# Gated linear attention and GLU in one kernel: chunks of 128 tokens, and the low parts on VectorE

## The chip, the cores and the metric

The kernel runs on one core of a Trainium2 chip. The metric is the device time of one execution of the whole program, in microseconds (us). The kernel before takes 612.56 us, the median of three runs (611.88 to 612.68).

The core's engines each follow their own list of instructions and wait for one another by semaphores: TensorE (PE in the profile; its weight loads have a row of their own, PEld), VectorE (DVE), ScalarE (ACT), GpSimd (POOL), and SyncE (SP), which here only starts transfers. SBUF is the memory that all engines use; PSUM holds what TensorE accumulates, in eight banks of 128 partitions x 512 words.

## The reference

Four sequences of 768 tokens, eight heads of 48 channels. Each head carries a 48 x 48 state through its sequence; what comes out is the input of a gated linear unit.

```python
for t in range(S):
    state = alpha[:, :, t, :, None] * state + np.einsum('bhd,bhe->bhde', k[:, :, t], v[:, :, t])
    y[:, :, t] = np.einsum('bhd,bhde->bhe', q[:, :, t], state)
...
x = attn_out.transpose(0, 2, 1, 3).reshape(B * S, H * D)      # 3072 x 384
gate = 1.0 / (1.0 + np.exp(-(x @ w_gate)))                    # 384 x 1536
val = x @ w_val
return (gate * val @ w_out)                                   # 1536 x 384
```

All inputs are float32. The kernel receives the weights as float64 words with the same values.

## The kernel before

**Groups, steps and units.** The 3072 tokens are six groups of T = 512. The GLU of a group has 12 **steps**, one for each 128 of the 1536 inner channels, so there are 72 (`step`, L507). The attention of a group has four **units**, one for each pair of heads, so there are 24 (`unit`, L340). A pair of heads lies on the 128 partitions, one head in the lower and one in the upper half, 48 of 64 partitions each.

**A step.** Every product with weights is done three times, on a high and a low part of each factor in a rounded 32-bit format (`products`, L198; `PAIRS`): high x high, high x low, low x high. TensorE makes pg and pv (gate and value, nine matmuls of 512 columns each, L202), and later po (L526), nine more: six with hh, three with hl. Between them ACT makes the sigmoid of pg (L512, tile sg), DVE multiplies it with pv (L513, into sg), ACT rounds that to the high part hh (L515), and POOL subtracts for the low part hl (L518). PSUM has one bank for pg, one for pv, three for po (they accumulate over the 12 steps of a group) and three, called at, for the units.

**A unit.** It works in chunks of C = 64 tokens, so a group has CH = 8 of them. The input tile (in, one DMA from `rows`) holds decay factors, k and q by channel; va and vb hold v of the two heads. DVE scans the decays backwards (G, L357) and forwards (F, L361), with small operations between (L359, L360, L363); POOL makes k x G (L365), and DVE and POOL make q x F (L375, tiles xa and xb); ACT sums |F| for an overflow flag (L377). TensorE then does four things, 16 matmuls each unless said otherwise: it turns k over (L387, a product with the identity; ACT copies it out as kn, L392), makes the scores of each chunk (L399; DVE masks them, L415), makes what each chunk adds to the state (L406; DVE chains the states chunk by chunk, L431), and makes the outputs. In groups 2 to 5 each output is one matmul (L470) over a stacked factor: the masked scores and q x F lie in two halves of the partitions of xa and xb, and v and the scaled states (L439, POOL) in those of va and vb. In groups 0 and 1 (`apart`) the two terms are separate matmuls (L457, L461). ACT and DVE make the parts of y (L476, L477), and a DMA puts them into x (L485).

**Weights.** A weight piece comes in by DMA and is split in six operations (`weight_piece`, L298): ACT scales the upper words (L312) and makes exponent and upper fraction bits in the 16-bit half words (L313), DVE takes the sign by half words (L315) and shifts in the lower bits (L317), ACT makes the high part (L319), POOL the low part (L321). There are 25 pieces, three for the first of the 12 weight blocks and two for each other one.

**What sets the order.** All of this goes into a planner (`Plan`, L42) as parts: engine, modelled time, key, and what it reads and writes. `order` (L71) plays the parts through by these times and picks, on each engine, the ready part with the lowest key. What it finds is each engine's fixed order of instructions. The keys follow the step at which a part is wanted. Rings of buffers (`Ring`, L127) set how far a unit can run ahead: two input tiles, two hh and hl, one sg. WARM = 60 matmuls (L497) without use stand at the start.

Of the kernel before, what the change touches and what calls it, by code (L numbers as in the profile page):

```python
# [8 lines left out]
F32 = mybir.dt.float32  # L9
# [11 lines left out]
C = 64  # L21
# [20 lines left out]
class Plan:  # L42
# [13 lines left out]
    def add(self, engine, time, key, fn, reads=(), writes=()):  # L56
# [12 lines left out]
        self.parts.append((engine, time, key, fn, deps))  # L69

    def order(self):  # L71
# [12 lines left out]
        begun, memory, busy = [None] * len(self.parts), 0.0, {}  # L84
        for _ in self.parts:
            best = None
            for e, ns in waiting.items():
                if not ns:
                    continue
                t = max(free[e], min(ready_at[n] for n in ns))  # L90
                n = min((n for n in ns if ready_at[n] <= t + 1e-9), key=lambda n: (self.parts[n][2], n))
                if best is None or t < best[0]:
                    best = (t, n)
# [14 lines left out]
            free[engine] = done  # L108
            if engine != "tensor" and data is not None:
# [48 lines left out]
RATE = 225e3  # L158
# [10 lines left out]
def act(n):  # L169
    return 0.09 + n / 1180  # L170
# [35 lines left out]
def chunked(ctx, tc, rows, vc, weights_in, out, const, ident, flags, weights, within):  # L206
# [45 lines left out]
    r_va = ring("va", 2, CH, D, early=[borrow("w8", CH, D) for _ in range(2)])  # L252
    r_vb = ring("vb", 2, CH, D, early=[borrow("w8", CH, D) for _ in range(2)])
# [5 lines left out]
    r_kn = ring("kn", 1, CH, D, early=[borrow("w6", CH, D) for _ in range(2)])  # L259
    r_sd = ring("sd", 1, CH, D, early=[borrow("w6", CH, D) for _ in range(2)] + [borrow("w7", CH, D)])  # L260
    r_yt = ring("yt", 2, 2, T, dtype=F32R)
    r_xa = ring("xa", 2, T, early=[borrow("x1", T), borrow("w7", T)])
    r_xb = ring("xb", 2, T, early=[borrow("x1", T), borrow("w7", T)])
# [22 lines left out]
    for half in range(2):  # L286
        m = mask[half * C:(half + 1) * C]
        nc.gpsimd.affine_select(out=m, in_=m, pattern=[[1, C]], compare_op=ALU.is_ge,
                                fill=0.0, base=0, channel_multiplier=-1)
    for r, lo in ((r_va, 0), (r_vb, C)):  # L290
        for _, t in r.tiles + r.early:
            nc.vector.memset(t[lo:lo + C], 0.0)
# [5 lines left out]
    def weight_piece(f, key):  # L298
        cuts = (0, DM, 2 * DM, WF) if f == 0 else (0, WF // 2, WF)
        over = before(f"w{f}") if f >= 6 else []  # L300
        for i, (lo, hi) in enumerate(zip(cuts, cuts[1:])):
# [4 lines left out]
            half = raw.bitcast(U16).rearrange("p m (w h) -> p m w h", h=2)  # L306
            ru, rl = (rn, "u"), (rn, "l")
            up = upper.bitcast(F32)
# [3 lines left out]
            plan.add("scalar", act(n), kk, lambda up=up: nc.scalar.activation(out=up, in_=up, func=AF.Copy, scale=2.0 ** -112), writes=[ru])  # L312
            plan.add("scalar", 0.09 + n / 500, kk, lambda half=half: nc.scalar.activation(  # L313
                out=half[:, :, 0, 0], in_=half[:, :, 0, 1], func=AF.Copy, scale=2.0 ** -13, bias=2.0 ** -15 - 0.5), writes=[rl])
            plan.add("vector", 0.1 + n / 770, kk, lambda half=half: nc.vector.tensor_scalar(  # L315
                out=half[:, :, 0, 1], in0=half[:, :, 1, 1], scalar1=0x8000, scalar2=None, op0=ALU.bitwise_and), [ru], [rl])
            plan.add("vector", 0.07 + n / 860, kk, lambda upper=upper, lower=lower: nc.vector.scalar_tensor_tensor(  # L317
                out=lower, in0=upper, scalar=3, in1=lower, op0=ALU.logical_shift_left, op1=ALU.bitwise_or), [ru], [rl])
            plan.add("scalar", act(n), kk, lambda lower=lower, lo=lo, hi=hi: nc.scalar.copy(  # L319
                out=weights.tile(f)[:, 0, lo:hi], in_=lower.bitcast(F32)), [rl], [("wh", f, i), *over])  # L320
            plan.add("gpsimd", pool_(n), kk, lambda lower=lower, lo=lo, hi=hi: nc.gpsimd.tensor_tensor(  # L321
                out=weights.tile(f)[:, 1, lo:hi], in0=lower.bitcast(F32), in1=weights.tile(f)[:, 0, lo:hi], op=ALU.subtract),
                [rl, ("wh", f, i)], [("w", f, i)])
# [16 lines left out]
    def unit(u, g, p, t):  # L340

        n, nch = T, CH
        apart = u < 2 * NP
        bank = r_bank if u < NP else r_at
        inn, tin = r_in.next()
        for lo, hi, marks in ((0, A_K, "a"), (A_K, WIDTH, "rk")) if u < 2 else ((0, WIDTH, "ark"),):
# [228 lines left out]
    for g in range(NG):  # L575
        if 2 <= g + 1 < NG:
            units(g + 1)
# [156 lines left out]
```

## Time and profile before

| | |
|---|---|
| median of three runs | 612.56 us |
| profiled execution | 612.03 us |
| its span, first to last instruction | 610.3 us |
| TensorE clock granted, mean over the span | 0.988 of full |
| moved by DMA | 52.94 MB, mean 87 GB/s |
| of the chain of work that ended last | PE 83%, DVE 8%, POOL 3%, ACT 3%, issue 2% |

The busy time of an engine in the page counts its instructions, and for TensorE the ends of matmuls are modelled. The page also cuts the span into 40 slices of 15.26 us and gives the busy share of each in tenths:

```profile
PE   7985989889999999999999999999999999999995
DVE  7875799799961535534534535525535312101111
ACT  1374775856342122132122132122132122212121
```

One reads them as a course of events: TensorE is not quite full for the first ten slices, while DVE and ACT split the weights and the units of the first two groups are made; after that TensorE is full and the others repeat a pattern of three slices.

### The profile page before, as it was taken

What the parts mean: (1) busy time and instruction counts of PE and PEld (TensorE: products, weight loads), DVE (VectorE), ACT (ScalarE), POOL (GpSimd) and SP (SyncE); (2) the same over time, 40 slices, a digit from 0 to 9 for tenths busy, and PEclk for the clock granted to TensorE, in tenths of its full rate; (3) what the DMA queues carried; (4) which work ended last, traced back from release to release, by engine and by line L of the source; (5) the groups of instructions that cost most, each with busy time, mean ns of one, the idle gap of its engine ahead of it and who ended that gap; (6) DMA issues with size and microseconds to landing.
All of it is one profiled execution on the core that took longest, in us unless ns stands there. A gap on an engine that the chain in (4) does not pass through costs nothing.

```text
span 610.3 us, 12631 instructions
## 1 busy us (share of the span) xinstructions
PE 583.8 (96%) x5334; PEld 464.9 (76%) x5334; DVE 307.3 (50%) x536; ACT 200.1 (33%) x331; POOL 266.4 (44%) x241
## 2 busy tenths in 40 slices
PE   7985989889999999999999999999999999999995
PEld 3754767677788888888888888888888888888784
DVE  7875799799961535534534535525535312101111
ACT  1374775856342122132122132122132122212121
POOL 4556586687771425425434425425424312212110
PEclk9997999999999999999999999999999999999998
DMA  8466465463440130240330240330340110110001
GB/s 269 131 178 231 133 188 183 147 197 116 145 118 0 53 92 8 85 144 6 87 92 6 88 144 2 91 92 2 93 143 2 40 27 1 38 41 0 1 2 58
DMA packets 17107, 52.94 MB, mean 87 GB/s; under 512 B 2832, under 2 KB 5904, under 8 KB 17040
## 3 DMA queue, kind: packets, MB, share of 16 engines
q1 hardware_dynamic: 17040, 52.03, 28.3%
q8 instruction: 44, 0.72, 0.5%
q14 instruction: 23, 0.19, 0.1%
HBM read 37.86 MB, written 4.72 MB: 70 GB/s over the span
## 4 chain that ended last, share of the span: by engine, by line
PE 83%; DVE 8%; POOL 3%; ACT 3%; issue 2%; DVEq 0%; POOLq 0%; ACTq 0%
PE po L526 23%; PE pg L202 22%; PE pv L202 22%; PE at L399 3%; PE at L387 3%; PE at L470 3%; PE at L406 3%; DVE first_w L315 1%; DVE first_w L317 1%; PE pv L497 1%; POOL w L321 1%; ACT raw L313 1%; DVE G L357 1%; DVE raw L315 1%; POOL xa L375 1%
## 5 line engine op out<-in xcount | busy, mean ns | idle before, releaser
L202 PE MATMUL pg<-x,w 128*128 128x512 f32 x648 | 166.0, 400 | 10.0 <-ACT sg L512 4.8
L518 POOL TENSOR_TENSOR hl<-sg,hh 128x512 fp32r<-128x512 f32 x71 | 97.8, 1377 | 156.5 <-ACT hh L515 155.4
L202 PE MATMUL pv<-x,w 128*128 128x512 f32 x648 | 160.2, 391 | 0.0
L202 PEld LDWEIGHTS pg<-x,w 128*128 128x128 f32 x648 | 122.4, 191 | 40.1 <-ACT sg L512 4.9
L513 DVE TENSOR_TENSOR sg<-pv,sg 128x512 f32<-128x512 f32 x72 | 49.5, 687 | 194.8 <-PE pv L202 189.2
L202 PEld LDWEIGHTS pv<-x,w 128*128 128x128 f32 x648 | 120.9, 188 | 26.6 <-DVE sg L513 0.8
L526 PE MATMUL po<-hh,w 128*128 128x512 f32 x432 | 116.7, 404 | 0.3 <-ACT hh L515 0.3
L512 ACT ACTIVATE sg<-pg 128x512 f32<-128x512 f32 x72 | 43.6, 605 | 187.8 <-PE pg L202 181.0
L526 PEld LDWEIGHTS po<-hh,w 128*128 128x128 f32 x432 | 78.6, 188 | 19.4 <-ACT hh L515 1.2
L515 ACT CAST hh<-sg 128x512 fp32r<-128x512 f32 x72 | 44.8, 622 | 113.1 <-DVE sg L513 113.1
L526 PE MATMUL po<-hl,w 128*128 128x512 f32 x216 | 62.9, 398 | 2.2 <-POOL hl L518 2.2
L365 POOL TENSOR_TENSOR in<-in,G 128x512 f32<-128x512 f32 x22 | 28.3, 1288 | 70.3 <-DVE G L357 64.2
L357 DVE TENSOR_TENSOR_SCAN G<-in,d1g 128x512 f32<-128x512 f32 x22 | 30.4, 1384 | 52.4 <-DMA in<-in_rows_dram 52.3
L375 POOL TENSOR_TENSOR xb<-in,F 64x512 f32<-64x512 f32 x16 | 26.9, 1684 | 57.3 <-PE at L470 54.3
L526 PEld LDWEIGHTS po<-hl,w 128*128 128x128 f32 x216 | 40.2, 188 | 13.3 <-POOL hl L518 3.8
L431 DVE SCALAR_TENSOR_TENSOR st<-st,dec,at 128x48 f32<-128x48 f32 x176 | 46.2, 263 | 7.4 <-PE at L406 2.0
L361 DVE TENSOR_TENSOR_SCAN F<-in,d1f 128x512 f32<-128x512 f32 x22 | 37.0, 1680 | 1.5
L321 POOL TENSOR_TENSOR w<-raw,w 128x576 fp32r<-128x576 f32 (+1 forms) x14 | 23.5, 1682 | 10.8 <-ACT w L319 10.5
L476 ACT CAST yt<-at 128x512 fp32r<-128x512 f32 x22 | 13.0, 592 | 46.2 <-PE at L470 40.7
L387 PE MATMUL at<-ident,in 48*64 48x48 f32 x704 | 24.9, 220 | 1.9 <-POOL in L365 1.9
L399 PE MATMUL at<-xa,in 48*64 48x64 f32 x416 | 24.2, 226 | 2.6 <-POOL xa L375 1.4
L387 PEld LDWEIGHTS at<-ident,in 48*64 48x64 f32 x704 | 22.2, 134 | 5.8 <-POOL in L365 2.8
(134 smaller groups left out, 648.2 us busy)
## 6 DMA issues: line engine op xcount, KB each, us to landing
in<-in_rows_dram SPq DMA_DIRECT2D x20, 772.5 KB, 5.5
x<-yt SPq DMA_DIRECT2D x36, 192.0 KB, 5.3
raw<-in_w_dram SPq DMA_DIRECT2D x12, 576.0 KB, 4.5
first_w<-in_w_dram SPq DMA_DIRECT2D x10, 576.0 KB, 4.6
out_dram<-raw SPq DMA_DIRECT2D x18, 256.0 KB, 2.4
va<-in_vc_dram SPq DMA_DIRECT2D x22, 96.0 KB, 3.0
vb<-in_vc_dram SPq DMA_DIRECT2D x22, 96.0 KB, 2.8
first_w<-in_rows_dram SPq DMA_DIRECT2D x2, 772.5 KB, 8.1
```

The lines of the kernel that those rows point to most:

```text
L202: nc.tensor.matmul(out=dst, lhsT=lhs(a, i), rhs=rhs(b, i), start=(n == 0 and i == 0), stop=(n == len(todo) - 1 and i == NK - 1))
L357: plan.add("vector", scan(n), t["G"], lambda: nc.vector.tensor_tensor_scan(out=G[:, ::-1], data0=az[:, n:0:-1], data1=d1g, initial=0.0, op ...
L361: plan.add("vector", scan(n), t["G"] + 0.01, lambda: nc.vector.tensor_tensor_scan(out=F, data0=az[:, 0:n], data1=d1f, initial=0.0, op0=ALU ...
L375: plan.add(e, vec(n) if e == "vector" else pool_(n), t["q"], lambda x=x, lo=lo, hi=hi, e=e: getattr(nc, e).tensor_tensor(out=x[lo:hi], in0 ...
L387: nc.tensor.matmul(out=pk[C * (1 - j):C * (2 - j), c * D:(c + 1) * D], lhsT=kt[r, c * C:(c + 1) * C], rhs=ident[r, C * j:C * j + D], start ...
L399: nc.tensor.matmul(out=pa[C * (1 - j):C * (2 - j), cs], lhsT=kt[r, cs], rhs=(xb if j and not apart else xa)[r, cs], start=True, stop=True)
L431: nc.vector.scalar_tensor_tensor(out=st[:, c + 1, :], in0=st[:, c, :], scalar=dec[:, c:c + 1], in1=pd[:, c * D:(c + 1) * D], op0=ALU.mult, ...
L512: plan.add("scalar", act(T), s - 100, lambda: nc.scalar.activation(out=sg, in_=got["g"][1][:, 0:T], func=AF.Sigmoid), [got["g"][0]], [sgn])
L513: plan.add("vector", vec(T), s - 100, lambda: nc.vector.tensor_tensor(out=sg, in0=got["v"][1][:, 0:T], in1=sg, op=ALU.mult), [got["v"][0]] ...
L515: plan.add("scalar", act(T), s - 100, lambda: nc.scalar.copy(out=hh, in_=sg), [sgn], [hhn])
L518: plan.add(e, vec(T) if last else pool_(T), s - 100, lambda: getattr(nc, e).tensor_tensor(out=hl, in0=sg, in1=hh, op=ALU.subtract), [sgn, ...
L526: nc.tensor.matmul(out=pso_now[m][1][:, 0:T], lhsT=weights.part("o", b, f)[:, m * P:(m + 1) * P], rhs=h[a][:, 0:T], start=(f == 0 and i == ...
```

## The change

- **Chunks of 128 tokens** (C = 128, four in a group). The two heads stay 64 partitions apart, which is now a constant of its own, R. The host lays out `rows` and `vc` accordingly, so that v of both heads comes in one DMA, into one tile. Since a chunk now fills all 128 rows, the outputs can't be stacked: all units make them as two terms (L427, L431), 16 matmuls, and groups 1 to 5 put them into pg's bank. k is turned over by four transposes of 128 x 128 (L370). The scores are eight matmuls, each head into a bank of its own (L381), with one mask operation a head (L394). The states are four (L409). q x F is written in place into the input tile (L359). The memsets that cleared halves of va and vb go.
- **Weight splitting.** ACT makes whole words (L308) where it made half words; DVE takes sign and lower bits in two operations of one kind by words (L311); the low part moves from POOL to DVE (L315).
- **Gated product.** DVE writes it into pv's PSUM bank (L474), ACT makes hh from there (L476), and hl is made by DVE from there (L477) where POOL made it from SBUF. So pv's bank is held until hl is made.
- **Planner and order.** `Plan` gets a flag for parts that don't run at the same time as GpSimd's, and a modelled DMA rate of 280e3 instead of 225e3. A unit's code is cut into three pieces with `yield`, and the loop puts the last piece of a unit between the first two of the next, so that TensorE's work for both can stand at one place, once every three steps.

```diff
-C = 64
+C = 128
+R = 64
...
-    def add(self, engine, time, key, fn, reads=(), writes=()):
+    def add(self, engine, time, key, fn, reads=(), writes=(), port=False):
...
-                t = max(free[e], min(ready_at[n] for n in ns))
-                n = min((n for n in ns if ready_at[n] <= t + 1e-9), key=lambda n: (self.parts[n][2], n))
+                begin = {n: max(ready_at[n], port if self.parts[n][5] else 0.0) for n in ns}
+                t = max(free[e], min(begin.values()))
+                n = min((n for n in ns if begin[n] <= t + 1e-9), key=lambda n: (self.parts[n][2], n))
...
-RATE = 225e3
+RATE = 280e3
...
-            plan.add("scalar", 0.09 + n / 500, kk, lambda half=half: nc.scalar.activation(
-                out=half[:, :, 0, 0], in_=half[:, :, 0, 1], func=AF.Copy, scale=2.0 ** -13, bias=2.0 ** -15 - 0.5), writes=[rl])
-            plan.add("vector", 0.1 + n / 770, kk, lambda half=half: nc.vector.tensor_scalar(
-                out=half[:, :, 0, 1], in0=half[:, :, 1, 1], scalar1=0x8000, scalar2=None, op0=ALU.bitwise_and), [ru], [rl])
-            plan.add("vector", 0.07 + n / 860, kk, lambda upper=upper, lower=lower: nc.vector.scalar_tensor_tensor(
-                out=lower, in0=upper, scalar=3, in1=lower, op0=ALU.logical_shift_left, op1=ALU.bitwise_or), [ru], [rl])
+            plan.add("scalar", act(n), kk, lambda most=most, lower=lower: nc.scalar.activation(
+                out=lower, in_=most, func=AF.Copy, scale=2.0 ** -13, bias=2.0 ** -15 - 0.5), writes=[rl])
+            for a, x, y in ((0x80000000, ALU.bitwise_and, ALU.bitwise_or), (3, ALU.logical_shift_left, ALU.bitwise_or)):
+                plan.add("vector", 0.07 + n / 860, kk, lambda upper=upper, lower=lower, a=a, x=x, y=y: nc.vector.scalar_tensor_tensor(
+                    out=lower, in0=upper, scalar=a, in1=lower, op0=x, op1=y), [ru], [rl], port=True)
...
-            plan.add("gpsimd", pool_(n), kk, lambda lower=lower, lo=lo, hi=hi: nc.gpsimd.tensor_tensor(
+            plan.add("vector", vec(n), kk, lambda lower=lower, lo=lo, hi=hi: nc.vector.tensor_tensor(
                 out=weights.tile(f)[:, 1, lo:hi], in0=lower.bitcast(F32), in1=weights.tile(f)[:, 0, lo:hi], op=ALU.subtract),
...
+                nc.tensor.transpose(out=pk[:, c * P:(c + 1) * P], in_=kT[:, c * P:(c + 1) * P], identity=ident)
...
+                for j in range(2):
+                    cs, r = slice(c * C, (c + 1) * C), slice(R * j, R * j + D)
+                    nc.tensor.matmul(out=pas[j][1][:, cs], lhsT=kT[r, cs], rhs=qT[r, cs], start=True, stop=True)
...
+        pyn, py = pas[0] if u < NP else r_pg.tiles[0]
+
+        def outputs():
+            for c in range(nch):
+                for j in range(2):
+                    cs, r = slice(c * C, (c + 1) * C), slice(R * j, R * j + D)
+                    nc.tensor.matmul(out=py[r, cs], lhsT=sd[r, c, :], rhs=qT[r, cs], start=(c == 0), stop=False)
+            for c in range(nch):
+                for j in range(2):
+                    cs = slice(c * C, (c + 1) * C)
+                    nc.tensor.matmul(out=py[R * j:R * j + D, cs], lhsT=v[:, c, j], rhs=As[j][1][:, cs],
+                                     start=False, stop=(c == nch - 1))
...
-        plan.add("vector", vec(T), s - 100, lambda: nc.vector.tensor_tensor(
-            out=sg, in0=got["v"][1][:, 0:T], in1=sg, op=ALU.mult), [got["v"][0]], [sgn])
-        plan.add("scalar", act(T), s - 100, lambda: nc.scalar.copy(out=hh, in_=sg), [sgn], [hhn])
+        pvn, pv = got["v"][0], got["v"][1][:, 0:T]
+        plan.add("vector", vec(T), s - 100, lambda: nc.vector.tensor_tensor(out=pv, in0=pv, in1=sg, op=ALU.mult), [sgn], [pvn])
         last = s == NG * NF - 1
-        e = "vector" if last else "gpsimd"
-        plan.add(e, vec(T) if last else pool_(T), s - 100, lambda: getattr(nc, e).tensor_tensor(out=hl, in0=sg, in1=hh, op=ALU.subtract), [sgn, hhn], [hln])
+        plan.add("scalar", act(T), s - 100, lambda: nc.scalar.copy(out=hh, in_=pv), [pvn], [hhn])
+        plan.add("vector", vec(T), s - 100, lambda: nc.vector.tensor_tensor(out=hl, in0=pv, in1=hh, op=ALU.subtract), [pvn, hhn], [hln])
...
+    for s in range(NG * NF):
+        step(s)
+        if s in finished:
+            u = finished[s]
+            following = begin(u + 1) if u + 1 < NG * NP else iter((None, None))
+            next(following)
+            next(now, None)
+            next(following)
+            now = following
```

**TensorE, where a unit cuts in.** TensorE's order in the kernel before, at step 7 of the second group (its pg and pv take w7), where a unit of the third group stands. in1 is the input of the next unit; at0 to at2 are the units' banks.

```order
L202 MATMUL pg0_122<-x1_1020,w7_1267 128x512 x9
L202 MATMUL pv0_123<-x1_1020,w7_1267 128x512 x9
L470 MATMUL at1_120<-xa0_90,va0_80 48x64
L470 MATMUL at1_120<-xb0_92,vb0_82 48x64 x2
...
L387 MATMUL at2_121<-ident_58,in1_79 64x48 x16
L399 MATMUL at0_119<-xa1_91,in1_79 64x64
L399 MATMUL at0_119<-xb1_93,in1_79 64x64 x2
...
L526 MATMUL po0_124<-hh0_115,w6_1166 128x512 x2
...
L202 MATMUL pg0_122<-x1_1020,w8_1326 128x512 x9
L202 MATMUL pv0_123<-x1_1020,w8_1326 128x512 x9
L406 MATMUL at2_121<-va1_81,kn0_86 48x48
```

The same place in the changed kernel, with sd the scaled states and A00, A10 the masked scores of the two heads:

```order
L206 MATMUL pg0_120<-x1_698,w7_752 128x512 x9
L206 MATMUL pv0_121<-x1_698,w7_752 128x512 x9
L370 MATMUL at0_117<-ident_58,in1_79 128x128 x4
L381 MATMUL at1_118<-in1_79 128x128
L381 MATMUL at2_119<-in1_79 128x128
...
L427 MATMUL pg0_120<-in0_78,sd0_85 48x128 x8
L431 MATMUL pg0_120<-A00_88,v0_80 48x128
L431 MATMUL pg0_120<-A10_90,v0_80 48x128
...
L386 MATMUL at0_117<-v1_81,kn0_84 48x48 x8
L485 MATMUL po0_122<-hh0_113,w6_719 128x512 x2
...
L206 MATMUL pv0_121<-x1_698,w8_847 128x512 x9
L206 MATMUL pg0_120<-x1_698,w8_847 128x512 x9
```

A unit's work stood at two places of three steps (outputs, turning and scores at one, the adds after the next step's products); now all of it stands at one, and since the outputs hold pg's bank, the next step makes pv first.

**VectorE, while weights are split.** VectorE's order in the kernel before, up to the first gated product (L513); raw1 and first_w11 are weight pieces on their way.

```order
L361 SCALAR_TENSOR_TENSOR F0_96<-in0_78,d1f_104 128x512
L315 TENSOR_SCALAR raw1_85<-raw1_85 128x576
L317 SCALAR_TENSOR_TENSOR raw1_85<-raw1_85 128x576
L315 TENSOR_SCALAR first_w11_76<-first_w11_76 128x576
L415 TENSOR_TENSOR xb1_93<-at0_119,mask_106 128x512
L317 SCALAR_TENSOR_TENSOR first_w11_76<-first_w11_76 128x576
L513 TENSOR_TENSOR sg0_114<-pv0_123,sg0_114 128x512
```

And in the changed kernel, around its first gated product (L474), where L315 writes the low part of the fourth weight block, w3:

```order
L311 SCALAR_TENSOR_TENSOR raw0_82<-raw0_82 128x576
L353 SCALAR_TENSOR_TENSOR F0_94<-in0_78,d1f_102 128x512
L315 TENSOR_TENSOR w3_544<-first_w11_76,w3_544 128x576
...
L474 TENSOR_TENSOR pv0_121<-pv0_121,sg0_112 128x512
L409 SCALAR_TENSOR_TENSOR st0_107<-st0_107,dec0_98,at0_117 128x48 x3
L315 TENSOR_TENSOR w3_544<-raw0_82,w3_544 128x576
L477 TENSOR_TENSOR hl0_115<-pv0_121,hh0_113 128x512
```

Each weight piece has three operations here instead of two, the gated product is followed by hl, and more weight blocks stand ahead of the first gated product.

**VectorE in the full stage.** Its order in the kernel before, in the second group, from the masks of a unit over the scan of the one after to the next gated products:

```order
L415 TENSOR_TENSOR xa0_90<-at2_121,mask_106 64x512
L415 TENSOR_TENSOR xb0_92<-at2_121,mask_106 64x512
L357 SCALAR_TENSOR_TENSOR G0_94<-in0_78,d1g_105 128x512
L513 TENSOR_TENSOR sg0_114<-pv0_123,sg0_114 128x512
L431 SCALAR_TENSOR_TENSOR st0_109<-st0_109,dec0_100,at1_120 128x48 x8
L359 TENSOR_TENSOR G00_98<-G0_94,tiny_107 128x8
L363 TENSOR_TENSOR dec2_102<-in0_78,G0_94 128x8
L360 RECIPROCAL d1f_104<-G00_98 128x8
L361 SCALAR_TENSOR_TENSOR F0_96<-in0_78,d1f_104 128x512
```

And in the changed kernel:

```order
L474 TENSOR_TENSOR pv0_121<-pv0_121,sg0_112 128x512
L394 TENSOR_TENSOR A01_89<-at1_118,mask_104 128x512
L394 TENSOR_TENSOR A11_91<-at2_119,mask_104 128x512
L477 TENSOR_TENSOR hl1_116<-pv0_121,hh1_114 128x512
L409 SCALAR_TENSOR_TENSOR st1_108<-st1_108,dec1_99,at0_117 128x48 x4
L437 TENSOR_TENSOR yt0_86<-pg0_120,yt0_86 128x512
L349 SCALAR_TENSOR_TENSOR G0_92<-in0_78,d1g_103 128x512
...
L352 RECIPROCAL d1f_102<-G00_96 128x4
L474 TENSOR_TENSOR pv0_121<-pv0_121,sg0_112 128x512
L353 SCALAR_TENSOR_TENSOR F0_94<-in0_78,d1f_102 128x512
```

The scan G and its small operations still stand ahead of a gated product (L474), the scan F behind it; hl now lies between, and only after it is pv's bank free.

More of the change, by code (lines that the diff above doesn't have):

```diff
@@ L108, in order @@
             free[engine] = done
+            if self.parts[n][5]:
+                port = done
             if engine != "tensor" and data is not None:
@@ L285, in chunked @@
     nc.gpsimd.memset(mask, 1.0)
[L286 to L292, printed above, removed]
+    nc.gpsimd.affine_select(out=mask, in_=mask, pattern=[[1, C]], compare_op=ALU.is_ge, fill=0.0, base=0, channel_multiplier=-1)
     def weight_piece(f, key):
@@ L305, in weight_piece @@
             upper, lower = raw[:, :, 1], raw[:, :, 0]
-            half = raw.bitcast(U16).rearrange("p m (w h) -> p m w h", h=2)
+            most = raw.bitcast(U16).rearrange("p m (w h) -> p m w h", h=2)[:, :, 0, 1]
             ru, rl = (rn, "u"), (rn, "l")
-            up = upper.bitcast(F32)
             kk = key + 0.5 * i
@@ L396, in scores @@
+        def scores():
             for c in range(nch):
-                for j in ((0, 1), (1, 0))[c % 2]:
-                    cs, r = slice(c * C, (c + 1) * C), slice(C * j, C * j + D)
-                    nc.tensor.matmul(out=pa[C * (1 - j):C * (2 - j), cs], lhsT=kt[r, cs],
-                                     rhs=(xb if j and not apart else xa)[r, cs], start=True, stop=True)
-        def adds(pd):
+                for j in range(2):
+                    cs, r = slice(c * C, (c + 1) * C), slice(R * j, R * j + D)
+                    nc.tensor.matmul(out=pas[j][1][:, cs], lhsT=kT[r, cs], rhs=qT[r, cs], start=True, stop=True)
@@ L403, in adds @@
+        def adds():
             for c in range(nch):
-                for j in ((0, 1), (1, 0))[c % 2]:
-                    r = slice(C * (1 - j), C * (2 - j))
-                    nc.tensor.matmul(out=pd[C * j:C * j + D, c * D:(c + 1) * D], lhsT=kn[r, c], rhs=(vb if j else va)[r, c],
+                for j in range(2):
+                    nc.tensor.matmul(out=pk[R * j:R * j + D, c * D:(c + 1) * D], lhsT=kn[:, c, R * j:R * j + D], rhs=v[:, c, j],
                                      start=True, stop=True)
-        pan, pa = bank.next()
@@ L423, in unit @@
+        yield
         st, sn = sts[p], ("st", p)
@@ L573, in chunked, with last_step @@
+    def last_step(u):
+        return NF * (u // NP - 1) + 10 - 3 * (NP - 1 - u % NP)
+    for u in range(NP):
+        for _ in begin(u):
+            pass
     for f in range(NF):
         weight_piece(f, -58.0 if f == 0 else -20.0 if f == 1 else f - 3.0)
-    for g in range(NG):
-        if 2 <= g + 1 < NG:
-            units(g + 1)
-        for s in range(g * NF, (g + 1) * NF):
-            step(s)
+    now = begin(NP)
+    next(now), next(now)
+    finished = {last_step(u): u for u in range(NP, NG * NP)}
```

182 lines of the change are left out of this document (66 added, 116 removed).

## The prediction

> **What bounds the kernel now.** The page's busy shares come first, then the busy times in stages; the columns of the second view are window, its length, and for PE, PEld, DVE, ACT and POOL the busy us (x instructions), then the granted clock, the DMA share and GB/s.
>
> ```profile
> PE 583.8 (96%) x5334; PEld 464.9 (76%) x5334; DVE 307.3 (50%) x536; ACT 200.1 (33%) x331; POOL 266.4 (44%) x241
> 0.00:41.00 41.00, 35.99 (x700) 24.07 (x700) 33.43 (x80) 15.39 (x27) 22.50 (x36) 1.00 0.65 198
> 41.00:56.00 15.00, 6.42 (x57) 4.58 (x54) 8.85 (x11) 6.91 (x10) 7.72 (x7) 0.91 0.87 273
> 56.00:163.00 107.00, 100.90 (x1112) 78.20 (x1113) 95.62 (x129) 73.15 (x101) 76.78 (x54) 0.97 0.48 150
> 163.00:592.00 429.00, 429.00 (x3432) 349.07 (x3427) 166.62 (x314) 101.68 (x188) 158.10 (x144) 1.00 0.19 55
> ```
>
> From 163 to 592 us PE is busy 429.00 of 429.00 at full clock: there only PE's own work counts. In 56 to 163 DVE is busy 95.62 of 107, so two engines share the limit. Before 41 PE runs mostly warm-up products. The chain of work that ended last (start us, us, what) shows what PE does in the full stage; the last rows are from the chain's start and end.
>
> ```profile
> 197.23 1.08 PE at L399 x32
> 198.31 2.30 PE po L526 x9
> ...
> 204.73 0.85 PE at L406 x32
> 205.58 2.30 PE po L526 x9
> 207.88 2.08 PE pg L202 x9
> 209.96 2.04 PE pv L202 x9
> 212.00 2.11 PE po L526 x9
> ...
> 218.23 1.03 PE at L470 x32
> 219.26 1.06 PE at L387 x32
> 220.32 0.95 PE at L399 x32
> 221.27 2.30 PE po L526 x9
> ```
> ```profile
> 55.66 2.93 PE pg L202 x6
> ...
> 142.92 1.03 PE at L457 x32
> 143.94 1.03 PE at L461 x32
> ...
> 603.27 0.02 issue
> ```
>
> A product step is pg 2.08 + pv 2.04 + po 2.11 = 6.23 us. From 198.31 to 221.27 are 22.96 us, three steps (18.69) and one attention unit: 4.27 us, of which 1.03 + 1.06 + 0.95 + 0.85 = 3.89 are its own and 2 x 0.19 come back as a longer po (2.30 against 2.11) at each of the two places where it cuts in. A unit of the first two groups has the outputs as L457 and L461, 2.06 instead of 1.03; at 1.06 + 1.08 + 0.85 + 2.06 it is about 5.05 (L399 takes 0.13 more where it follows products).
>
> Now the profiled span as a sum. Step 1 begins at 55.66. From there: all pg and pv of steps 1 to 71 and 72 po, 71 x 6.23 + 2.11 = 444.4; the rest of unit 4 (4.0), units 5 to 7 (15.15), units 8 to 23 (16 x 4.27 = 68.3), together 87.5; from PE's end at 603.27 to 610.3, 7.0. The sum is 594.6, so **15.7 us are waits and cold clock**, nearly all between 56 and 163. Around the span lie 612.03 - 610.3 = 1.73 us, and the profiled run is 0.53 under the median of 612.56.
>
> **The change on PE, unit by unit.** A unit's 64 matmuls become 4 transposes, 8 scores, 8 adds and 16 outputs. Each present matmul leaves two records, and the two heads' records run beside each other: 32 records of 64 columns (L399) take 0.95, or 59 ns a pair; 64 columns with 128 rows (L470, L457, L461) take 1.03, or 64 ns; 48 columns (L406, 0.85 less the 0.13 after products) 45 ns. The slope from 48 to 64 is 0.9 ns a column, so a pair of 128 columns is estimated at 59 + 58 = 117 ns, by proportion to L470 at 129.
> - Scores: 8 pairs of 128 columns, 0.94. This needs the two heads, on different row halves but all columns, to run beside each other; in every present row the heads also differ in columns. If they run one after another it is 1.88.
> - Outputs: 16 pairs of 128 columns, 1.87 to 2.06; taken 1.95. The stacked form that gave 1.03 is gone.
> - Adds: 8 pairs of 48 columns, 0.36; with the slope of 128 rows 0.40.
> - Transposes: no such row. Below, 4 x 59 ns = 0.24; above, 4 x 0.218, one record's whole length without overlap, plus 0.13 = 1.0. Taken 0.6, in between, since the shortest would need the 128-column loads to vanish.
>
> ```profile
> L399 PE MATMUL at<-xb,in x256: 218/218/267, 150.6 to 496.6; 48*64 48x64 f32 x128
> ```
>
> The row is minimum/median/maximum ns of one record. The sum is 0.94 + 1.95 + 0.38 + 0.6 = 3.87, and with one cut of 0.19, 4.06 where 4.27 stood. The upper bounds (no serial scores) give 0.94 + 2.06 + 0.40 + 1.0 + 0.19 = 4.6, the lower ones 0.94 + 1.87 + 0.36 + 0.24 + 0.19 = 3.6. I take 4.3, nearer the upper, since all four shapes are new and a wait inside the cut comes on top. Units 8 to 23: 68.8; units 5 to 7, with no cut in a po, 3 x 4.1 = 12.3; the rest of unit 4, 3.5. Together **84.6 against 87.5, -2.9**; at 4.6 it would be +3, at 3.6 -17.
>
> The rule in the Trainium skill's page "TensorE: Matmul & The Clock Gate", Part 4, is that a PE transpose of 128x128 took about 275 ns in one kernel. By that figure four would be an estimated 1.1 us, the unit 4.6 and the sum 6 us later. No run so far shows a transpose here.
>
> **On DVE, ACT and POOL.** The first table groups DVE's work in 56 to 163 us (count | busy us, mean ns | idle before); then single costs, over the whole run.
>
> ```profile
> L317 DVE SCALAR_TENSOR_TENSOR raw<-raw 128x576 uint32<-128x576 uint32 x11 | 13.4, 1217 | 0.2
> L315 DVE TENSOR_SCALAR first_w<-first_w 128x576 uint16<-128x576 uint16 x9 | 13.2, 1467 | 3.3 <-ACT first_w L313 3.3
> L315 DVE TENSOR_SCALAR raw<-raw 128x576 uint16<-128x576 uint16 x11 | 12.3, 1115 | 0.3
> L317 DVE SCALAR_TENSOR_TENSOR first_w<-first_w 128x576 uint32<-128x576 uint32 x9 | 11.3, 1250 | 0.1
> L431 DVE SCALAR_TENSOR_TENSOR st<-st,dec,at 128x48 f32<-128x48 f32 x40 | 10.4, 260 | 2.0 <-PE at L406 1.1
> L357 DVE TENSOR_TENSOR_SCAN G<-in,d1g 128x512 f32<-128x512 f32 x5 | 9.7, 1945 | 0.0
> L361 DVE TENSOR_TENSOR_SCAN F<-in,d1f 128x512 f32<-128x512 f32 x5 | 8.6, 1719 | 0.1
> ```
> ```profile
> 45.33 0.76 DVE L317 SCALAR_TENSOR_TENSOR raw<-raw 128x576 uint32<-128x576 uint32 x1
> L359 DVE TENSOR_TENSOR G<-G,tiny x23: 156/766/1250, 6.4 to 460.6; 128x8 f32<-128x8 f32 x23
> L357 DVE TENSOR_TENSOR_SCAN G<-in,d1g x22: 1192/1224/2460, 5.1 to 456.6; 128x512 f32<-128x512 f32 x22
> L513 DVE TENSOR_TENSOR sg<-pv,sg x72: 659/692/734, 55.6 to 599.4; 128x512 f32<-128x512 f32 x72
> L518 DVE TENSOR_TENSOR hl<-sg,hh x1: 693/693/693, 600.8 to 600.8; 128x512 fp32r<-128x512 f32 x1
> ```
>
> An undisturbed L317 is 0.76, an undisturbed G scan 1.22; here they average 1.2 and 1.95, while L513, which reads PSUM, is never stretched: VectorE and GpSimd hold each other up on SBUF. In this window the weights' two DVE operations cost 50.2. After the change 20 half pieces take three operations of 0.76 (the low part as L518 on DVE, 0.69 for 512 columns, 0.78 for 576): 46. G and F fall to 12.2 from 18.3 if POOL, which loses 25 weight subtractions and 71 of L518 (97.8 of its 266.4 us), stays out of the way; the states halve (-5.2), the small ones lose some 3; added are 11 x 0.69 = 7.6 for hl and five more masks, 3.5. DVE's demand goes from about 103 to about 93, and by the order four of the 20 half pieces are already done before the first gated product: 84. What POOL still has per unit (two products of 1.3, small copies) can stretch that by up to 18. The ACT pass L313 lies between today's 1.52 and L312's 0.74; I take 0.74, because only its 16-bit output changes to 32, and DVE waits 3.3 us for it now. Hence I let **the waits shrink from 15.7 to 12.5, -3.2**; bounds 7 and 19.
>
> **Before step 1.** Fifteen more weight operations stand ahead of the first gated product (11.4 us), 16 state updates of 0.26 and 3.1 us of memsets go, four masks (2.8) come: +6.9 net, into the 7.6 + 6.1 us in which DVE is idle up to 56. Against that, PE waited here once for the sigmoid:
>
> ```profile
> PE pg L202 <- ACT sg L512: 4.8, 1, 4.8
> ```
>
> ACT stood behind an |F| pass whose POOL product was late; in the new order that pass stands behind the second sigmoid. I take **-1** for this stage, between -5 and +4.
>
> **Holding pv longer.** In a product step hl on DVE now frees the pv bank. From a unit's start (0): transposes and scores to 1.5, first half of the outputs to 2.5, which frees the input buffer; the load lands 5.5 later:
>
> ```profile
> in<-in_rows_dram SPq DMA_DIRECT2D x20, 772.5 KB, 5.5
> ```
>
> That is 8.1; the G scan, which stands ahead of the next gated product on DVE, and three small operations end at 9.8. PE meanwhile ends the unit at 3.9, po 6.2, pv 8.2, pg 10.3; sigmoid 0.60; the product can start at 11.0, so the scan is hidden by 1.2. Then 0.69, F 1.22 beside ACT's 0.62, hl 0.69: 13.7. PE wants pv again after po and pg, at 14.5: 0.8 spare. Cost nothing; with that cover gone every us late is paid once per unit, 15 times. In steps without a unit the chain 0.69 + 0.62 + 0.69 is 2.0 against 4.19.
>
> **Sum.** 610.3 - 2.9 - 3.2 - 1 = 603.2 in span; with 1.73 604.9, and with the 0.53 up to the median **605.5 us**.
>
> **The rivals.**
> 1. *The two heads' scores run one after another* on PE, since both now write all 128 columns. For it: no row shows row halves alone overlapping. Against: L470 shows column halves alone doing so at 64 ns against 59. Price 0.94 a unit x 20 = 18.8, less what the waits of the first stage hide: 605.5 + 16.5 = 622. It decides against the kernel once a pair costs some 165 ns instead of 117 (8 x 0.048 x 20 = 7.7). Chance 0.13; slower.
> 2. *The gated product comes late*: landing over 8 us, or F stretched as in the table, makes hl miss pv by 1 us, 15 times: 605.5 + 14 = 619.5. The load's 5.5 speaks against. Chance 0.09; slower.
> 3. *Each transpose runs its whole length*, 0.218 each and its first 0.13 more, and the outputs cost their 2.06: 4.6 a unit, 605.5 + 20 x 0.3 = 611.5. Chance 0.12: within 0.2% mostly. This is the side on which the page's 275 ns lies.
> 4. *The estimates are too dear*: 3.9 a unit and waits of 11 give 605.5 - 20 x 0.4 - 1.5 = 596. Chance 0.14.
>
> **How the numbers follow.** My forecast, some 599 to 610, has 0.52. Faster than 611.3: 0.52 + 0.14 + a third of rival 3 = 0.69; within 0.2%, which is about what a measurement of this kernel can tell from no change, 0.07; slower 0.24, with rivals 1 and 2. The range of 595 to 619 leaves out about 0.18, mostly rival 1.
>
> **What would show it.** In the full stage: three steps and a unit in 22.8 to 22.9 us, one cut per unit, pairs of scores starting some 5 to 10 ns apart. On DVE: G, F and L317's successors near 1.22 and 0.76, and the last weight subtraction some 30 us before 160. The product step 12 should begin near 152 to 156 instead of 163.42. Scores of 1.9 a unit, a wait of pv for hl after the units, or a step 12 that still begins after 160 would make it wrong.

## The result and the profile after

The changed kernel takes **596.64 us**, the median of four runs (595.59 to 598.77), where the kernel before took 612.62 (four runs, 611.88 to 616.23): a ratio of 0.9732, 95% interval 0.9685 to 0.978. The profiled execution took 598.77, the longest of the four, with a span of 597.1. The forecast was 605.5: the direction was right, the gain 16.0 us instead of 7.1.

First the page's busy shares and the same stages as before (window, length, busy us of PE, PEld, DVE, ACT, POOL, then granted clock, DMA share, GB/s):

```profile
PE 572.8 (96%) x3638; PEld 459.5 (77%) x3638; DVE 317.8 (53%) x536; ACT 182.6 (31%) x331; POOL 72.0 (12%) x112
0.00:41.00 41.00, 34.99 (x307) 21.32 (x308) 34.11 (x65) 15.61 (x31) 19.48 (x31) 0.92 0.80 262
41.00:56.00 15.00, 10.54 (x69) 7.92 (x70) 13.15 (x21) 12.27 (x19) 2.95 (x5) 0.75 0.62 190
56.00:163.00 107.00, 100.48 (x637) 79.03 (x637) 81.95 (x138) 54.93 (x96) 19.63 (x23) 0.98 0.43 136
```

POOL's work fell from 266.4 to 72.0 us, and DVE between 56 and 163 from 95.62 to 81.95, though it took over the low parts that POOL had made. The clock before 56 is lower than it was.

The chain of waits, from one unit to the next (start us, us, what), and two rows from steps without units:

```profile
230.67 0.44 PE at L370 x4
231.11 1.09 PE at L381 x16
232.20 1.01 PE pg L427 x16
233.21 1.01 PE pg L431 x16
234.22 0.36 PE at L386 x16
234.58 2.29 PE po L485 x9
...
240.96 2.10 PE po L485 x9
243.06 2.04 PE pg L206 x9
245.10 2.04 PE pv L206 x9
247.14 2.10 PE po L485 x9
...
257.25 2.31 PE po L485 x9
...
517.28 2.10 PE po L485 x9
...
560.59 2.10 PE po L485 x9
```

Seven steps from 517.28 to 560.59 give 6.187 us each (before, five from 542.86 to 574.02 gave 6.23). From 234.58 to 257.25 are 22.67 us, three steps and a unit: the unit costs 4.11 (before 4.27). So the sum of the prediction can be filled in, each of the two profiled executions against its own span:

| term | forecast | measured |
|---|---|---|
| up to step 1 | -1 | 55.66 to 54.68: -1.0 |
| products, 71 x step + po | 0 | 444.4 to 441.4: -3.0 |
| units 4 to 23 | -2.9 | 87.5 to 81.2 (16 x 4.11, 3 x 4.1 as forecast, rest of unit 4 3.1): -6.3 |
| waits and cold clock (what is left) | -3.2 | 15.7 to 12.4: -3.3 |
| after TensorE's end | 0 | 7.0 to 7.4 (597.1 - 589.68): +0.4 |
| span | -7.1 | 610.3 to 597.1: -13.2 |

The other 2.8 us between -13.2 and the medians' -16.0 are scatter: the profiled run lay 2.1 above its median here, 0.6 below it before.

### The profile page after: what moved, and what is told of

Read it like the earlier page. It is cut to its first block, busy times and chain, and to the rows that moved or that the text cites. A ratio compares the mean times of both kernels' runs of the same rounds, so it can differ in the third digit from the quotient of the medians.

```text
span 597.1 us, 8948 instructions
## 1 busy us (share of the span) xinstructions
PE 572.8 (96%) x3638; PEld 459.5 (77%) x3638; DVE 317.8 (53%) x536; ACT 182.6 (31%) x331; POOL 72.0 (12%) x112
## 4 chain that ended last, share of the span: by engine, by line
PE 87%; DVE 6%; DMA 3%; ACT 1%; issue 1%; SPq 0%; POOL 0%; DVEq 0%; POOLq 0%; ACTq 0%
PE po L485 24%; PE pv L206 24%; PE pg L206 23%; PE at L381 4%; PE pg L427 3%; PE pg L431 3%; PE pv L457 2%; PE at L370 1%; DMA in<-in_rows_dram 1%; DMA x<-yt 1%; PE at L386 1%; DMA raw<-in_w_dram 1%; DVE w L315 1%; DVE raw L311 1%; DVE first_w L311 1%; DVE G L349 1%
## 5 line engine op out<-in xcount | busy, mean ns | idle before, releaser
L206 PE MATMUL pg<-x,w 128*128 128x512 f32 x648 | 163.9, 398 | 10.1 <-DVE yt L437 5.0
L206 PE MATMUL pv<-x,w 128*128 128x512 f32 x648 | 161.9, 394 | 0.6 <-DVE hl L477 0.5
L206 PEld LDWEIGHTS pg<-x,w 128*128 128x128 f32 x648 | 123.5, 192 | 38.5 <-DVE yt L437 6.0
L474 DVE TENSOR_TENSOR pv<-pv,sg 128x512 f32<-128x512 f32 x72 | 50.3, 698 | 187.8 <-PE pv L206 161.0
L206 PEld LDWEIGHTS pv<-x,w 128*128 128x128 f32 x648 | 122.4, 190 | 27.7 <-DVE hl L477 1.6
L476 ACT CAST hh<-pv 128x512 fp32r<-128x512 f32 x72 | 42.4, 588 | 83.6 <-DVE pv L474 83.6
L477 DVE TENSOR_TENSOR hl<-pv,hh 128x512 fp32r<-128x512 f32 x72 | 49.1, 683 | 20.3 <-ACT hh L476 20.3
L416 POOL TENSOR_TENSOR sd<-st,dec 128x192 f32<-128x192 f32 x22 | 13.1, 596 | 292.8 <-DVE st L409 287.7
L357 POOL TENSOR_TENSOR in<-in,G 128x512 f32<-128x512 f32 x22 | 29.8, 1354 | 63.3 <-DVE G L349 61.7
L394 DVE TENSOR_TENSOR A<-at,mask 128x512 f32<-128x512 f32 x42 | 27.2, 686 | 13.4 <-PE at L381 13.3
L409 DVE SCALAR_TENSOR_TENSOR st<-st,dec,at 128x48 f32<-128x48 f32 x88 | 23.1, 263 | 12.0 <-PE at L386 10.0
L311 DVE SCALAR_TENSOR_TENSOR raw<-raw 128x576 uint32<-128x576 uint32 (+1 forms) x28 | 24.0, 864 | 0.7 <-ACT raw L308 0.7
L381 PE MATMUL at<-in 48*128 48x128 f32 x336 | 24.4, 284 | 0.0
L374 ACT COPY kn<-at 128x512 f32<-128x512 f32 x22 | 12.9, 586 | 36.5 <-PE at L370 36.5
L381 PEld LDWEIGHTS at<-in 48*128 48x128 f32 x336 | 20.4, 187 | 4.7 <-issue 4.7
```

Source lines behind the costliest of these rows:

```text
L206: nc.tensor.matmul(out=dst, lhsT=lhs(a, i), rhs=rhs(b, i), start=(n == 0 and i == 0), stop=(n == len(todo) - 1 and i == NK - 1))
L357: plan.add("gpsimd", pool_(n), t["kt"], lambda: nc.gpsimd.tensor_tensor(out=kT, in0=kT, in1=G, op=ALU.mult), [gn, (inn, "r")], [(inn, "k")])
L381: nc.tensor.matmul(out=pas[j][1][:, cs], lhsT=kT[r, cs], rhs=qT[r, cs], start=True, stop=True)
L394: plan.add("vector", vec(n), t["mask"], lambda pa=pa, A=A: nc.vector.tensor_tensor(out=A.rearrange("p (c t) -> p c t", t=C), in0=pa[:, 0:n ...
L474: plan.add("vector", vec(T), s - 100, lambda: nc.vector.tensor_tensor(out=pv, in0=pv, in1=sg, op=ALU.mult), [sgn], [pvn])
L476: plan.add("scalar", act(T), s - 100, lambda: nc.scalar.copy(out=hh, in_=pv), [pvn], [hhn])
```

## The experiments

Each run is timed beside the kernel before on the same chip (medians 612.7 to 614.8, single runs 611 to 618), so ratios are compared. "Step 12" is the start of its first product in the profiled run; "rest" is from there to the end of the last matmul's record (before 163.3 and 440.1, changed 152.7 and 437.2). A rest can be compared where the parts stand in the same order; another order can move a unit's work across step 12.

**The base.** The changed kernel again.

> The changed kernel once more, unchanged, as the base of the other runs and for a second profile. Its four times so far were 595.59 to 598.77, and the profiled one was the longest. If that scatter lies in the stage before step 12, this profile has step 12 begin at some other time than 152.74 us while the distance from there to the end stays within 0.3 us of 444.4 us (597.1 - 152.74); if it lies in the full stage, step 12 begins within 0.5 us of 152.74 and the distance differs.

598.23 us (597.76 to 598.58), ratio 0.9747 (0.9716 to 0.9778); step 12 at 152.4, rest 437.1. Of the 0.6 us between the two profiled executions 0.36 lie ahead of step 12 and 0.05 in the rest; the two are too near each other to show where the 3 us of scatter arise.

**Two cuts a unit.** `Y=y + 0.53` becomes `Y=y + 1.51`.

> In the changed kernel the adds of a unit of groups 2 to 5 get the key of the kernel before, so that they cut in after the next step's products, at a place of their own. Theory: each place where a unit cuts in costs 0.13 to 0.19 us on TensorE (a product or a po that starts behind other work takes longer), so 16 units lose 2.1 to 3.0 us and three steps with a unit take 22.80 to 22.86 instead of 22.67. Rival: the cost belongs to the shapes and not to the place; then three steps with a unit stay within 0.03 us of 22.67 and the time within 0.5 us of the base.

602.94, ratio 0.9827 (0.9797 to 0.9857). Its chain of waits:

```profile
232.80 2.30 PE po L485 x9
235.10 2.06 PE pg L206 x9
237.16 2.04 PE pv L206 x9
239.20 0.49 PE at L386 x16
239.69 2.30 PE po L485 x9
...
255.84 2.31 PE po L485 x9
```

There are 23.04 us from 232.80 to 255.84, 0.37 more than with one cut: 0.20 for the second po, 0.13 for the adds (0.49, not 0.36), 0.04 in pg. The theory holds, at twice the price: rest is 442.3, 5.2 longer, of which 1.8 come back since step 12 begins at 150.6 with the adds moved behind it. With two cuts the unit would cost 4.48, more than the 4.27 of the kernel before: on TensorE the new shapes pay only because they stand at one place.

**hl on GpSimd again**, from sg in SBUF, in the changed kernel; and the reverse, the gated product of the change alone in the kernel before.

> In the changed kernel the gated product goes back to sg in SBUF, and hl back to GpSimd. Theory 1: a step lost 0.05 us (6.235 to 6.185, all of it in pg, 2.08 to 2.04) because hl no longer runs on GpSimd from SBUF beside pg; then pg is 2.08 again, the full stage gains 71 x 0.045 = 3.2 us, DVE's SBUF operations in the first stage are stretched again by GpSimd, and the time is some 600 to 604. Rival: pg's 0.04 comes from the layout or the units, and hl's place does not matter to it; then pg stays at 2.04 and the time is 596 to 599, by the first stage alone.

> The kernel before with the gated product's part of the change alone: product written to PSUM, hl made by DVE from there. Theory 1: pg falls from 2.08 to 2.04, 3.2 us over 71 steps, and in the stage of the weights GpSimd stretches DVE less while DVE has 0.69 us more to do per step, about even: some 607 to 610. Rival (pg's 0.04 comes from layout or units): pg stays 2.08, and the time is within 1.5 us of the kernel before.

Undone: 607.81, ratio 0.9897 (0.9868 to 0.9927), rest 437.6 with pg at 2.04, but step 12 at 162.1. Alone: 610.95, ratio 0.9954 (0.9931 to 0.9978), pg 2.08. In both the rival is right on pg: hl's place does not set it. On the time neither side was right: the undoing costs more than both said, and the gated product alone gains 0.5%, which comes between the two ranges. The cost of undoing lies ahead of step 12, where TensorE's waits for DVE (us in total, times, longest) are, with hl undone,

```profile
PE pg L206 <- DVE yt L437: 8.8, 1, 8.8
PE pv L206 <- DVE sg L473: 4.2, 1, 4.2
```

and 5.5 in all in the changed kernel. There the DVE groups between 56 and 163 (count | busy us, mean ns | idle before) read, with hl undone:

```profile
L311 DVE SCALAR_TENSOR_TENSOR first_w<-first_w 128x576 uint32<-128x576 uint32 x14 | 15.0, 1083 | 0.6 <-ACT first_w L308 0.6
L353 DVE TENSOR_TENSOR_SCAN F<-in,d1f 128x512 f32<-128x512 f32 x5 | 8.1, 1621 | 0.1
```

and in the changed kernel:

```profile
L311 DVE SCALAR_TENSOR_TENSOR first_w<-first_w 128x576 uint32<-128x576 uint32 x14 | 10.5, 752 | 0.0
L353 DVE TENSOR_TENSOR_SCAN F<-in,d1f 128x512 f32<-128x512 f32 x5 | 6.1, 1220 | 0.0
```

The same operations take 1083 and 1621 ns with GpSimd's subtractions, 752 and 1220 without. That this stretch makes the longer waits is argued, not shown: DVE's order differs too, and its busy time between 56 and 163 is nearly the same (82.44 and 81.95).

**Where sg, hh and hl lie.** These are four kernels with the same work, in which the three tiles are moved by an order of allocation or an unused tile. The table gives the remainder of hh's start address, in bytes within a partition, after division by 256; sg and hl have the same one.

```diff
 # e5: sg, hh, hl ahead of the last state tile; e16: of the last two
 # e6: 64 bytes ahead of sg, as here; e15: 192 bytes, 48 for 16
+    pad = sb.tile([P, 16], F32, name="pad")
     r_sg = ring("sg", 1, T)
```

> The kernel before, with sg, hh and hl allocated ahead of the last state tile, which moves them by 1728 bytes: their addresses go from multiples of 128 bytes to 64 past one, which is where the changed kernel has them. Nothing else moves but that state tile. Theory 1b: pg's 2.08 against 2.04 us in every step of the kernel before is set by where the factors of the preceding po lie; then pg is 2.04 and po 2.10 here, the full stage loses 3 us, and the time is some 610 to 611 on a chip where the kernel before takes 614. Rival: it comes from the units' matmuls or from the length of TensorE's program; then pg stays 2.08 and the time within 1 us of the kernel before.

> The changed kernel with 64 unused bytes ahead of sg, which puts sg, hh and hl on multiples of 128 bytes, as in the kernel before. Theory 1b: pg goes from 2.04 to 2.08 us and po from 2.10 to 2.11, and the time rises by 3 us, to some 601. Rival: both stay and the time is within 0.5 us of the changed kernel.

> The changed kernel with 192 unused bytes ahead of sg: hh and hl move from 214464 to 214656, which is 128 past a multiple of 256, as in the kernel before (221056), where 64 bytes more had put them on a multiple of 256. Theory A (place in 256 bytes): pg goes to 2.08 us in every step and TensorE's time from step 12 on from 437.1 to 439.5 or more. Rival: pg stays 2.04, and the place in 256 bytes is not what sets it.

> The kernel before with sg, hh and hl ahead of two state tiles: hh at 217600, a multiple of 256 (before 221056, 128 past one; in the earlier run 219328, 192 past one, pg 2.04). Theory A: pg is 2.04 and the time from step 12 on 2.5 us shorter than in the kernel before. Rival: pg is 2.08 again, since the place in 128 bytes is the same as before, and the changed kernel's layout has another reason.

| kernel | hh, remainder of 256 | pg | rest | ratio |
|---|---|---|---|---|
| before | 128 | 2.08 | 440.1 | 1 |
| e5, before moved | 192 | 2.04 | 438.3 | 0.9984 (0.996 to 1.0008) |
| e16, before moved | 0 | 2.04 | 438.3 | 0.999 (0.9968 to 1.0012) |
| changed | 192 | 2.04 | 437.1 | 0.9747 (0.9716 to 0.9778) |
| e6, changed moved | 0 | 2.04 | 437.3 | 0.9737 (0.9703 to 0.977) |
| e15, changed moved | 128 | 2.08 | 439.5 | 0.9763 (0.9732 to 0.9793) |

Theory 1b as first put (remainder of 128) fell with e6; by the remainder of 256, which e15 and e16 test, all six agree. In the changed kernel the slow place costs 2.4 us of rest. Its chain shows which products are slower:

```profile
257.14 2.30 PE po L486 x9
259.44 2.08 PE pv L206 x9
261.52 2.04 PE pg L206 x9
263.56 2.11 PE po L486 x9
265.67 2.08 PE pg L206 x9
267.75 2.04 PE pv L206 x9
```

It is the nine right behind po, pg in most steps and pv behind a unit. In the kernel before, taking the slow place away shortens the rest by 1.8 to 1.9 us. Whether the median falls by as much can't be told: 1.8 us would be a ratio of 0.997, which lies in both intervals, as 1 does. Step 12 begins at 166.3 to 166.5 in these two profiles, at a granted clock of 0.93 between 56 and 163 where the profile of the kernel before has 0.97; these are single executions, and why they differ is open.

**The bank of the outputs** of the second group (`pas[0] if u < 2 * NP`).

> The changed kernel, but the outputs of the second group's four units go to a bank of the units (as in the first group), not to pg's. Theory: the two waits of pg for the subtraction of y on DVE (5.0 us, the largest waits of TensorE after step 1) were made by this change's choice of bank; without it step 12 begins 3 to 5 us earlier and the time is 593 to 596 beside 598. Rival: DVE is the limit there and y comes as late; then x of the second group or the next scores are waited for instead, and the time is within 1.5 us of the changed kernel.

604.87, ratio 0.9859 (0.9827 to 0.989). The waits on y are gone, but TensorE waits 8.3 us for GpSimd's k x G (`PE at L370 <- POOL in L357`), and step 12 begins at 158.1. The rival was right that another wait takes its place, and 5 us too mild.

**k x G and q x F on DVE** (all units; the first two groups).

> The changed kernel with k x G, and q x F of the first two groups, made by DVE instead of GpSimd. In the changed kernel's trace the 128x4 product dec (0.15 us by its shortest) lasts 1.26 us wherever it starts beside GpSimd's k x G of 1.28, and ends with it. Theory: GpSimd's product holds DVE off for as long as it runs, so doing it on DVE for 0.69 costs DVE less than waiting 1.1 for it: dec falls to 0.15 to 0.2 everywhere, the chain from G to the scores gets 0.6 shorter, the waits for y shrink, and the time is 593 to 597 beside 598. Rival: DVE is loaded and the waits only happen to coincide; then dec stays long somewhere, DVE's demand grows by 0.7 to 1.4 a unit in the first stage, and the time is 599 to 602.

605.44, ratio 0.987 (0.9835 to 0.9905). The theory's mechanism shows and its sum falls; the rival's 599 to 602 was too mild as well. In the changed kernel (timeline: start, us), and the rows of dec by line (min/median/max ns), changed and then e12:

```profile
193.37 1.28 POOL L357 TENSOR_TENSOR in<-in,G 128x512 f32<-128x512 f32 x1 [2.65 <-DVE G L349]
193.40 1.26 DVE L355 TENSOR_TENSOR dec<-in,G 128x4 f32<-128x4 f32 x1
```

```profile
L355 DVE TENSOR_TENSOR dec<-in,G x22: 135/1265/1273, 5.0 to 466.2; 128x4 f32<-128x4 f32 x22
```

```profile
L355 DVE TENSOR_TENSOR dec<-in,G x22: 127/130/160, 5.0 to 474.1; 128x4 f32<-128x4 f32 x22
```

A product of four columns lasts as long as GpSimd's of 512 beside it, and 130 ns without. But k x G now stands in DVE's queue behind weights, and TensorE waits for it once for 8.1 us: step 12 at 160.0.

**The parts and the planner.** Weights and gated product in the kernel before (e8, whose order lets scaled states overwrite an input that an earlier unit's outputs still need, and e10, where the planner is told of that dependence); the chunks, with the units' new order and banks, without them, under the new rules (e9) and the old (e17); the whole change under the old rules (e11), or with one rule put back (e13, e14); the new DMA rate in the kernel before (e18).

```diff
-RATE = 280e3
+RATE = 225e3
...
-        self.parts.append((engine, time, key, fn, deps, port or engine == "gpsimd"))
+        self.parts.append((engine, time, key, fn, deps, False))
```

> The kernel before with both the weight splitting of the change (words, low parts on DVE) and its gated product, but with chunks of 64 and the old planner. My account gives the units and the steps on TensorE, which come with the chunks and the layout, some 9 us of the gain, and the first stage some 3 to 4 by DVE that GpSimd no longer stretches: this kernel should keep only the latter, 609 to 611 where the kernel before takes 614, with the scans at 1.2 and not 1.9 us between 56 and 163, and step 12 at 158 to 161. Rival: most of the first stage's gain needs the chunks (half the state updates, four conversions fewer ahead of step 1); then DVE has more to do than before and the time is 613 to 618.

> The kernel before with the weight splitting and the gated product of the change; the earlier run of this pair (615.5) let scaled states overwrite an input of an earlier unit's outputs, which the planner is now told of. Expected as that run showed, since the work is the same: 613 to 617, no gain without the chunks, step 12 at 164 to 168. If it falls to 609 or below, the first stage's gain is these two parts' alone and the earlier run misled.

> The changed kernel with three parts undone: sign by half words, low part of the weights on GpSimd, gated product in sg with hl on GpSimd. Chunks of 128, the units' new order and the planner stay. Theory (the parts need each other): the full stage keeps its gain (step 12 to the end of TensorE's work 437.1 to 437.6 us), but the first stage has GpSimd's subtractions back, which hold up DVE's operations on SBUF: scans at 1.6 to 2.0 us between 56 and 163, step 12 at 162 to 170, time 606 to 614. Rival (the chunks are what counts): halved state updates and fewer matmuls alone bring step 12 to within 3 us of 152.4, time 597 to 601.

> The changed kernel with the planner's rules of before: DMA rate 225e3, no part that waits for GpSimd's. Theory: the planner only moves parts of the first stage by fractions of a us each: 596 to 601, the distance from step 12 to the end unchanged at 437. Rival: the planner's model of GpSimd's hold on DVE is what puts the operations in an order that works; then step 12 is 5 us or more later, 603 or above.

> The changed kernel with only the planner's DMA rate put back to 225e3. Theory R (the rate): the order made with 280e3 counts on data earlier than they land, so parts of the first group's last unit stand behind weight pieces; putting the rate back gives all of the earlier run's gain: 589 to 592, step 1 before 48 us. Theory P (the rule on GpSimd): this run stays at 596 to 599 and the other one gains. If both gain 3 to 4, it is any other order, not one of the two.

> The changed kernel with only the planner's rule on GpSimd taken out, the DMA rate left at 280e3. Theory R: 596 to 600, step 1 at 52 to 55 us as in the changed kernel. Theory P: 589 to 592, step 1 before 48 us. If both runs gain 3 to 4, it is any other order.

> Chunks of 128 with the new order of the units, and nothing else of the change: signs by half words, low parts and hl on GpSimd, and the planner's old rules. With the new rules this was 602.9, where all parts together were 598; all parts with the old rules were 590.4. Theory (weights and gated product are worth the same under either set of rules, some 5 us, and the new rules cost some 7 in any kernel with chunks of 128): 594 to 598. Rival (the old rules suit the full change only, since the rules decide what stands beside GpSimd's work): 601 to 606.

> The kernel before with the planner's DMA rate of the change, 280e3, and nothing else. Theory (the higher rate plans for data earlier than they land): 615 to 619, with step 1 or step 12 later than 55.7 and 163 to 166. Rival (each order is a draw, and the rate is not wrong as such): within 2 us of the kernel before, on either side.

| | median us | ratio to before |
|---|---|---|
| weights and gated product, no chunks, old rules (e10; e8 615.53) | 613.43 | 1.0008 (0.9987 to 1.0028) |
| new DMA rate alone (e18) | 614.45 | 1.0005 (0.9976 to 1.0033) |
| chunks alone, new rules (e9) | 602.85 | 0.9827 (0.9792 to 0.9863) |
| chunks alone, old rules (e17) | 599.46 | 0.9741 (0.9706 to 0.9776) |
| all, new rules (the change, e1) | 598.23 | 0.9747 (0.9716 to 0.9778) |
| all, old DMA rate (e13) | 595.67 | 0.9704 (0.9673 to 0.9735) |
| all, no rule on GpSimd (e14) | 593.89 | 0.9669 (0.9637 to 0.9701) |
| all, old rules (e11) | **590.41** | **0.9627 (0.9591 to 0.9662)** |

Without the chunks the weights and the gated product together bring nothing, though the gated product alone brought 0.5% (e4). The chunks, with the units' new order and banks, bring 1.7 to 2.6%; with them, the other parts add 0.8% under the new rules and 1.1% under the old. The order that the planner's new rules give costs 0.9% (chunks alone) and 1.2% (all). Putting one back gains 0.43% (DMA rate, whose interval overlaps the change's) or 0.78% (GpSimd), which add up, so neither theory R nor P holds alone. The rate costs the kernel before nothing. Whether a rule is wrong as such or only the order that came out is not settled. Several forecasts here missed: e11 fell below both of its ranges, e17 came between its two, and e9 between them too, nearer to the rival (step 12 at 155.5). The change without them is the fastest kernel measured. Its stages before 56 us:

```profile
0.00:41.00 41.00, 35.36 (x344) 21.82 (x344) 32.43 (x66) 15.99 (x31) 17.87 (x32) 1.00 0.64 206
41.00:56.00 15.00, 10.79 (x71) 8.09 (x72) 12.84 (x20) 8.24 (x15) 6.23 (x6) 1.00 0.73 256
```

The last transfer of y of the first group goes out at 39.39 instead of 47.73 (the chains of waits), and step 1 begins at 45.5 instead of 54.7. The granted clock there is 1.00 and 1.00 where the change has 0.92 and 0.75; what each of the two contributes isn't parted.

## Why the prediction was right and wrong

Two terms of the sum were wrong in size: the unit's price and the step, which was taken as unchanged.

- **The unit's price** was worked out as 4.06 and then, by choice, taken as 4.3, "nearer the upper, since all four shapes are new and a wait inside the cut comes on top". This step failed: 4.11 was measured, and no wait came on top. It made 3.4 of the missing 8.9 us (16 x 0.19, and 0.4 in the rest of unit 4). By its shapes: transposes 0.44 (taken 0.6), scores 1.09 (0.94), outputs 2.02 (1.95), adds 0.36 (0.38); the single errors cancelled. Margin on a sum whose errors have both signs is a bias, not caution; it belonged in the range.
- **The step** had no term: "A product step is pg 2.08 + pv 2.04 + po 2.11" was carried over unchanged. It is 6.187, which made 3.0 us. The cause is the place of sg, hh and hl in memory, shown by e15 and, in the kernel before, by e5 and e16. That the change moved them to a faster place is luck: no term of the sum, and no part of the change, aims at it.
- **The first stage** was right in size, -1 and -3.2 against -1.0 and -3.3, and step 12 began at 152.7, inside "152 to 156". The stretch of DVE goes as said (scans at 1.22, L311 at 0.75 to 0.79), and the wait for the sigmoid falls from 4.8 to 0.9. But its going is worth little by itself: in e10 it is nearly gone (G 1.22, F 1.38 us), and step 12 begins at 165.1. With the chunks, the other parts bring step 12 from 155.5 (e9, F at 1.67) to 152.7 under the new rules, and from 155.5 (e17) to 145.8 (e11) under the old. The way from 163.3 to 155.5 came with the chunks and the units' order. DVE's demand, put at "about 103 to about 93", doesn't follow from its items, which add up to -7.4, and 103 stands in no row; that 84 was forecast and 81.95 came is luck in part. The agreement of the whole stage is a net one, too: the sum had no term for the planner's new rules, whose order takes back some 7 us there (e11 against e1). The waits that remained were new ones: 5.0 us of pg for y (`PE pg L206 <- DVE yt L437: 5.0, 2, 3.6`), since the outputs hold pg's bank.
- **Holding pv longer** cost nothing, as said: pv waited 0.5 us in all for hl. One load landed late (6.77 us in the chain after 210.24) and cost TensorE 0.38 us: pv began 0.24 late and took 0.14 longer.
- **The rivals.** Scores one after another: 8 pairs in 1.09 us are 136 ns a pair, dearer than the 117 taken, far from serial. Transposes at their whole length: a record lasts 272 ns, but four take 0.44 us. The Trainium skill's page "TensorE: Matmul & The Clock Gate", Part 4, gives about 275 ns for a transpose in one kernel; the trace agrees on one record and not on a row of them, which start 110 ns apart, so the estimate of 1.1 us by it did not apply. The rival with estimates too dear gave 596, the time that came, by other terms: units at 3.9 and waits of 11, where 4.11, 12.4 and a shorter step were measured.
- **The median** was put 0.53 above the profiled execution, as before. In four runs it lay 2.1 below it, and 0.1 above in e1: with executions that scatter by 3 us, the place of a profiled run among the others does not carry over.

## What to carry to other kernels

Put each term of a sum at its best value and the doubt into the range, not into the term. Price a scheduler's rules as a part of the change, with a run of the edits without them: here the order that came of rules meant to model the machine better took back a third of the gain. Before a step's duration is carried over, check whether the buffers that it reads will lie where they lay.

## What the runs showed of the hardware

- Where sg, hh and hl begin 128 bytes past a multiple of 256, the nine matmuls right behind po take 2.08 us instead of 2.04, although they read x and w; po takes 2.11 instead of 2.10, and the nine after those keep 2.04. This is shown for remainders 0, 128 and 192 only, with the three tiles moved together (e5 and e16 have 2.06 to 2.07 behind one po of each unit); the mechanism is open.
- A VectorE operation that reads two inputs from SBUF can last as long as the GpSimd operation beside it that does so too: in the changed kernel dec takes 1265 ns by its median, and 135 to 159 in the six of its 24 runs that are not beside GpSimd. The Trainium skill's page "SBUF — State Buffer", "Who interferes with whom", says that a VectorE instruction with two SBUF inputs contends with a GpSimd instruction that reads SBUF; the trace agrees. The gated product of the kernel before, which reads one input from PSUM, took 659 to 734 ns in 21 cases beside GpSimd and 659 to 693 in the others.
